# Widening float64 weights in an attention and expert kernel: the power of two taken from the moved upper word

## The chip, the cores and the metric

One core of a Trainium2 chip runs the whole program. The metric is the device time of one execution in microseconds; a kernel's time is the median of several executions.

## The reference, cut to what matters

Causal attention over 4 batches, 12 heads, 448 positions and 64 channels; then a block that multiplies by weights given in float64 (`w_theta`, `w_tok_r`, `w_tok_i`, `w_ch`); then a second attention over 4 experts with a gate.

```python
x = attention(q, k, v)                      # (4, 448, 768)
theta = x @ w_theta
zr, zi = x * np.cos(theta), x * np.sin(theta)
y = np.einsum('ts,bsd->btd', w_tok_r, zr) + np.einsum('ts,bsd->btd', w_tok_i, zi)
u = x + y
x = u + np.maximum(u @ w_ch, 0.0)
...
for e in range(4):                          # the second attention, expert by expert
    ye = softmax(causal(scale * (x @ wq[e]) @ (x @ wk[e]).T)) @ (x @ wv[e]) @ wo[e]
    out += (gate of e, among the best 2) * ye
```

The float64 weights reach the chip as pairs of 32-bit words. The products are made in two float32r parts, a rounded upper part (`hi`) and the rest (`lo`), with three matmuls for each product.

## The kernel before, in words

Work goes batch by batch, four times: the first attention (`attn1`, six pairs of heads), the dense block (`dense1`: theta, sine and cosine, transposes, mixing along the tokens, channel product, projections of the experts) and the second attention (`attn2`, two pairs of heads and the output product). The first attention of the next batch and the second one of the batch before are laid between the products of the dense block, so that TensorE has work while other engines prepare operands.

`Plan` (lines 126 to 478) sets the order. Every call of an engine in the kernel's text becomes a step with a cost (`Plan.cost`, lines 143 to 172), a due time and dependences. `Plan.issue` lays the steps out engine by engine by due time and by when inputs and buffers come free; for a step with several possible engines (`copy`, `combine`, `scale`, lines 284 to 296) it takes the one that would end first. What it emits is a fixed order for each engine. The table `K` (lines 489 to 493) holds the due times of the stages: `start` and `len0` for the first batch's dense block, `len` and `len3` for the others, `d1`, `g1` and `gap` for the attention beside them. A VectorE step of one source counts as fast, half the time for each column, by

```python
psum = any(v.root.psum for v in ins)
fast = name in ("tensor_scalar", "tensor_copy", "memset") and not psum and n >= 64
```

where `ins` are its inputs; the output is not looked at.

`widen` (lines 543 to 560) makes `hi` and `lo` of a tile of raw float64 words: 24 tiles of 384 columns for theta and channel weights (`c1`, shown as `c`), and 7 tiles of 448 for the token weights (`zt`, converted into `wt`). All of it is done in the first batch; `hi` and `lo` of the 24 go to DRAM (`scr`) and are loaded again by the later batches. Step by step: ScalarE scales the upper word (line 547), VectorE shifts it to its place and keeps the exponent (line 550) and adds the sign (line 552), both into `cmb`; VectorE masks the mantissa's bits in place (line 553); ScalarE makes of them a number from 1 to 2 in the PSUM tile `cv` (line 555); VectorE adds the lower word times 2^-52 (line 557); VectorE or POOL multiplies by the power of two (line 558); then come the rounded part and the difference (lines 559, 560), on whichever engine is first. `cv` is one PSUM bank, which the transposes ahead of the token mixing use too (lines 783 to 800).

In `dense1` each of the six theta products (`big`, line 747) fills one of two `mm` banks; VectorE's `zt<-mm` rows (lines 767, 768) empty it. Each of six token-mixing chains (lines 804 to 814) is 21 matmuls of `wt` with `zn`; `zn` is a transposed tile's rounded part and its residual, the VectorE row `zn<-cv,zn` of line 800. Names: `sc` scores, `pa`, `pc`, `zn` (in the first batch) their exponentials, `tp` and `ph` transposed ones, `hl` the two parts of an attention's output, `unit` the two parts of a weight tile. All instructions are recorded at line 478, so the trace is read by tiles.

Of the kernel before, what the change touches and what calls it, by code (L numbers as in the profile page):

```python
# [15 lines left out]
U32 = mybir.dt.uint32  # L16
AF = mybir.ActivationFunctionType
OP = mybir.AluOpType
# [13 lines left out]
LOWBIT = 2.0 ** -52  # L32
# [93 lines left out]
class Plan:  # L126
# [171 lines left out]
    def rank(self):  # L298
# [6 lines left out]
        for s in reversed(self.steps):  # L305
            if not s.users:
                continue
            path = s.lag if s.engine == "sync" else s.cost
            latest = min(u.due for u in s.users) - path * K["path"] - K["hop"]
            s.due = min(s.due, latest) if s.engine == "tensor" else latest  # L310

    def issue(self):
# [8 lines left out]
        def lag(e, d):  # L321
            if d == e:
                return OWN[e]
            return LATENCY[e] + K["slack"] + (50.0 if d == "tensor" else 0.0)

# [40 lines left out]
        def unpark(tag):  # L366
            for e, x in parked.pop(tag, ()):
                if not x[2].issued:
                    bisect.insort(avail[e], x, key=lambda x: x[:2])
# [5 lines left out]
        while count < len(self.steps):  # L375
# [13 lines left out]
            for e in order:  # L389
# [64 lines left out]
                for t in s.tiles:  # L454
                    t.left -= 1
                    if t.left == 0 and t.bufs:
                        heapq.heappush(free[t.tag], (done + K["war"], t.slot))
                        heapq.heappush(wake, done + K["war"])
                        unpark(t.tag)
# [21 lines left out]
class Engine:  # L481
# [3 lines left out]
    def __getattr__(self, method):  # L485
        return lambda *a, **kw: self._plan.add(self._name, method, *a, **kw)


K = {"path": 1.62, "hop": -40.0, "slack": 10.0, "war": 300.0, "ahold": 41390.0, "f1": 0.03, "f2": 0.79, "f3": 1.13,
# [4 lines left out]


# [1 line left out]
def dense_sparse_attention_kernel(ctx: ExitStack, tc: tile.TileContext, qk, v, w64, w32, wo, wvg, wtok, out):  # L497
# [6 lines left out]
    plan = Plan(nc, tc)  # L504
    pe, act, dve, pool, sp = (Engine(plan, n) for n in ("tensor", "scalar", "vector", "gpsimd", "sync"))
# [5 lines left out]
    def sbt(shape, dtype, tag):  # L511
        return plan.tile(sb, [P] + shape, dtype, tag, BUFS[tag])

    def pst(tag):
        return plan.tile(psp, [P, 512], F32, tag, PBUFS[tag], psum=True)
# [27 lines left out]
    def widen(raw, n, hi, lo):  # L543


        e_ = raw[:, :n, 1]
        act.activation(e_.f32(), e_.f32(), AF.Copy, scale=REBIAS)
        e_ = e_.bitcast(U32)
        p_ = sbt([S], F32, "cmb")[:, :n]
        dve.tensor_scalar(p_.bitcast(U32), e_, 3, 0x7F800000, op0=OP.logical_shift_left, op1=OP.bitwise_and)  # L550
        plan.claim(hi)
        dve.scalar_tensor_tensor(p_.bitcast(U32), e_, 0x80000000, p_.bitcast(U32), op0=OP.bitwise_and, op1=OP.bitwise_or)
        dve.tensor_scalar(e_, e_, 0xFFFFF, None, op0=OP.bitwise_and)
        x_ = pst("cv")[:, :n]
        act.activation(x_, e_, AF.Copy, scale=2.0 ** -20, bias=1.0)
        y_ = e_.bitcast(F32)
        dve.scalar_tensor_tensor(y_, raw[:, :n, 0].bitcast(U32), LOWBIT, x_, op0=OP.mult, op1=OP.add)
        plan.combine(p_, y_, p_, OP.mult, "vg")
        plan.copy(hi, p_, "sgv")
        plan.combine(lo, p_, hi.f32(), OP.subtract, "gv")  # L560

    def convert(src, n, hi, lo, tag="c1"):

        raw = sbt([S, 2], I32, tag)
        if src.dtype == F32:
            raw = raw.rearrange("p a b -> p (a b)").bitcast(F32)[:, :n]
            sp.dma_start(raw, src)
            plan.copy(hi, raw, "sgv")
            plan.combine(lo, raw, hi.f32(), OP.subtract)
        else:  # L570
            sp.dma_start(raw[:, :n].rearrange("p a b -> p (a b)"), src.bitcast(I32))
            widen(raw, n, hi, lo)
# [33 lines left out]
    def pair(raw, vts, gate, dest, due, gap, tag=lambda name: name):  # L606
# [18 lines left out]
        def part(j, c):  # L625
            return ps[j][:, SECS[c]:SECS[c] + 128 * (c + 1)]
# [18 lines left out]
        def norm(a, b_, items):  # L645
            dve.tensor_scalar(rec[:, a:b_], sums[:, a:b_], 1e-9, None, op0=OP.add)
            dve.reciprocal(rec[:, a:b_], rec[:, a:b_])
            if gate is not None:
                dve.tensor_tensor(rec[:, a:b_], rec[:, a:b_], gate[:, a:b_], op=OP.mult)
            for p, col in items:  # L650
                plan.scale(p, p, rec[:, col:col + 1])

        scores([2])
        norm(0, 2, [(part(j, 2), j) for j in range(2)])
        plan.due = due + K["f1"] * gap
        sc_ = pst("sc")
# [3 lines left out]
        norm(2, 7, [(pc[:, :S], 6)] + [(part(j, c), 2 * (2 - c) + j) for c in (1, 0) for j in range(2)])  # L660
        plan.due = due + K["f2"] * gap

# [280 lines left out]
    for b in range(B):  # L943
        gap = K["gap"] + (K["gap1"] if b == 1 else K["gap2"] if b == 2 else 0.0)
# [57 lines left out]
```

## Time and profile before

| what | value |
|---|---|
| median of 3 executions | 672.63 us (671.33 to 673.14) |
| the profiled execution, its own time | 672.36 us |
| its span, first to last instruction | 670.6 us |
| TensorE (PE) busy | 642.0 us, 96% of the span |
| VectorE (DVE) busy | 424.3 us, 63% |
| ScalarE (ACT) busy | 391.9 us, 58% |
| GpSimd (POOL) busy | 114.4 us, 17% |

A row's duration is longer than what it keeps its engine from the next: on VectorE the next row starts before the last one has ended. The start of the next row less the start of this one, on an engine that waits for nothing, is called its pitch below. TensorE's busy time counts overlapping matmuls once.

### The profile page before, as it was taken

Reading aid. Unit: us, or ns where it says so; the run is one execution under the profiler, and the core shown is the slowest. Engines: PE = TensorE matmul, PEld = TensorE weight load, DVE = VectorE, ACT = ScalarE, POOL = GpSimd, SP = SyncE. Lnnn points to the kernel's source line nnn. Section 1 sums busy time; section 2 is a strip of 40 time slices with the busy share of each in tenths; the row PEclk is TensorE's granted clock in tenths of the full one; section 3 lists DMA queues with packets and bytes.
Section 4 is the critical chain, followed back from the end, with each engine's and each line's share of the span. In section 5 each row is a group of like instructions: output and inputs, shape, how many; then the busy total and the mean of one; then the engine's idle time right before and its main releaser. Section 6 shows DMA issues by size and latency. Waiting matters only on the chain.

```text
span 670.6 us, 11048 instructions
## 1 busy us (share of the span) xinstructions
PE 642.0 (96%) x3728; PEld 520.5 (78%) x3728; DVE 424.3 (63%) x1325; ACT 391.9 (58%) x976; POOL 114.4 (17%) x224
## 2 busy tenths in 40 slices
PE   7997779999999999999999999999999999999987
PEld 5564567878797879887787778888878888998865
DVE  4999999999955685544526686553633567434251
ACT  5999788786813684444547677444555374105274
POOL 3542212222400120011001123001101012001010
PEclk9999789999999999999999999999999999999999
DMA  8846640355878624246546543415541750064253
GB/s 329 310 139 201 206 134 29 110 163 187 285 230 291 212 91 147 91 140 177 166 98 211 168 134 85 133 36 163 169 122 49 258 157 11 24 222 119 63 173 117
DMA packets 46184, 103.13 MB, mean 154 GB/s; under 512 B 4784, under 2 KB 16560, under 8 KB 46128
## 3 DMA queue, kind: packets, MB, share of 16 engines
q1 hardware_dynamic: 46128, 102.43, 48.0%
q8 instruction: 29, 0.48, 0.3%
q14 instruction: 27, 0.22, 0.1%
HBM read 81.15 MB, written 21.26 MB: 153 GB/s over the span
## 4 chain that ended last, share of the span: by engine, by line
PE 81%; DVE 8%; ACT 6%; DMA 3%; issue 1%; POOL 0%; ACTq 0%; SPq 0%; POOLq 0%; DVEq 0%
PE mm L478 53%; PE av L478 10%; PE sc L478 8%; PE tp L478 7%; PE cv L478 3%; DVE cmb L478 2%; ACT pa L478 2%; DMA unit<-scr 2%; ACT zn L478 1%; DVE zt L478 1%; DVE zn L478 1%; ACT ph L478 1%; DVE c L478 1%; ACT pc L478 1%; DVE pa L478 1%
## 5 line engine op out<-in xcount | busy, mean ns | idle before, releaser
L478 PE MATMUL mm<-zt,unit 128*128 128x448 f32 x720 | 161.4, 374 | 0.0
L478 ACT ACTIVATE pa<-pa,st 128x384 f32<-128x384 f32 (+2 forms) x265 | 126.6, 493 | 59.4 <-DVE st L478 55.3
L478 PEld LDWEIGHTS mm<-zt,unit 128*128 128x128 f32 x720 | 132.3, 188 | 16.6 <-issue 5.0
L478 PE MATMUL mm<-wt,zn 128*128 128x448 f32 x504 | 126.9, 380 | 0.6 <-ACT zn L478 0.5
L478 PE MATMUL mm<-hl,unit 128*128 128x448 f32 x432 | 102.8, 383 | 7.4 <-DVE zt L478 4.8
L478 PEld LDWEIGHTS mm<-wt,zn 128*128 128x128 f32 x504 | 90.0, 188 | 13.8 <-issue 3.1
L478 PEld LDWEIGHTS mm<-hl,unit 128*128 128x128 f32 x432 | 80.5, 192 | 21.2 <-DVE zt L478 6.6
L478 POOL TENSOR_SCALAR pa<-pa,st 128x384 f32<-128x384 f32 (+2 forms) x83 | 45.1, 551 | 267.6 <-DVE st L478 196.5
L478 DVE CUSTOM_DVE_ANT_0 pa<-sc,mask 128x384 f32<-128x384 f32 (+1 forms) x174 | 66.7, 418 | 36.8 <-PE sc L478 31.9
L478 ACT ACTIVATE ph<-tp 128x512 f32<-128x512 f32 x100 | 55.0, 593 | 29.8 <-PE tp L478 29.5
L478 PE MATMUL sc<-raw 64*128 64x384 f32 (+3 forms) x336 | 68.3, 432 | 1.4 <-DVE st L478 1.2
L478 PE MATMUL tp<-ident,pa 128*128 128x128 f32 x348 | 59.7, 279 | 5.0 <-POOL pa L478 5.0
L478 PEld LDWEIGHTS tp<-ident,pa 128*128 128x128 f32 x348 | 44.1, 143 | 12.9 <-POOL pa L478 6.6
L478 DVE TENSOR_TENSOR zn<-cv,zn 128x512 fp32r<-128x512 f32 (+1 forms) x48 | 29.8, 621 | 32.5 <-ACT zn L478 32.2
L478 PE MATMUL av<-ph,vt 128*64 128x448 f32 (+3 forms) x384 | 46.8, 386 | 2.2 <-ACT xt L478 2.2
L478 ACT ACTIVATE pc<-pc,st 128x448 f32<-128x448 f32 x51 | 34.1, 669 | 24.6 <-DVE st L478 23.9
L478 PEld LDWEIGHTS av<-ph,vt 128*64 128x64 f32 x384 | 25.4, 136 | 27.7 <-issue 13.3
L478 PEld LDWEIGHTS sc<-raw 64*128 64x128 f32 (+1 forms) x336 | 33.5, 187 | 12.4 <-issue 6.9
L478 PE MATMUL mm<-unit,zt 128*128 128x260 f32 (+1 forms) x264 | 36.9, 289 | 0.3 <-DMA unit<-scr 0.3
L478 PEld LDWEIGHTS mm<-unit,zt 128*128 128x128 f32 (+1 forms) x264 | 33.1, 183 | 4.2 <-issue 2.4
L478 ACT ACTIVATE zn<-cv 128x512 fp32r<-128x512 f32 (+1 forms) x34 | 18.5, 543 | 26.1 <-PE cv L478 25.9
L478 DVE SCALAR_TENSOR_TENSOR xt<-mm,xt 128x448 f32<-128x448 f32 x24 | 14.9, 620 | 29.3 <-PE mm L478 29.3
(121 smaller groups left out, 900.2 us busy)
## 6 DMA issues: line engine op xcount, KB each, us to landing
unit<-scr SPq DMA_DIRECT2D x96, 384.0 KB, 3.5
scr<-unit SPq DMA_DIRECT2D x32, 384.0 KB, 3.2
raw<-qk SPq DMA_DIRECT2D x24, 480.0 KB, 4.2
c<-w SPq DMA_DIRECT2D x24, 384.0 KB, 3.5
vt<-v SPq DMA_DIRECT2D x24, 256.0 KB, 2.9
unit<-scr SPq DMA_DIRECT2D x18, 260.0 KB, 3.1
c<-scr SPq DMA_DIRECT2D x18, 256.0 KB, 2.9
out<-cmb SPq DMA_DIRECT2D x18, 224.0 KB, 2.7
```

The source lines that it names most:

```text
L478: getattr(getattr(self.nc, engine), name)(*args, **kw)
```

## The change

In `widen` the shifted upper word keeps its mantissa bits too (mask `0x7FFFFFFF`), so that with the sign it is already the number without its lower word. Sign and exponent of it alone (mask `0xFF800000`) are a signed power of two, which VectorE writes to the PSUM tile `cv`. The lower word times 2^-52 times that power is added to the number. ScalarE's step on the mantissa (line 555 of before) is gone; VectorE's mask (line 553 of before) now reads `cmb` and writes `cv`.

```diff
-        dve.tensor_scalar(p_.bitcast(U32), e_, 3, 0x7F800000, op0=OP.logical_shift_left, op1=OP.bitwise_and)
+        dve.tensor_scalar(p_.bitcast(U32), e_, 3, 0x7FFFFFFF, op0=OP.logical_shift_left, op1=OP.bitwise_and)
...
-        dve.tensor_scalar(e_, e_, 0xFFFFF, None, op0=OP.bitwise_and)
         x_ = pst("cv")[:, :n]
-        act.activation(x_, e_, AF.Copy, scale=2.0 ** -20, bias=1.0)
+        dve.tensor_scalar(x_.bitcast(U32), p_.bitcast(U32), 0xFF800000, None, op0=OP.bitwise_and)
         y_ = e_.bitcast(F32)
-        dve.scalar_tensor_tensor(y_, raw[:, :n, 0].bitcast(U32), LOWBIT, x_, op0=OP.mult, op1=OP.add)
-        plan.combine(p_, y_, p_, OP.mult, "vg")
+        dve.scalar_tensor_tensor(y_, raw[:, :n, 0].bitcast(U32), LOWBIT, x_, op0=OP.mult, op1=OP.mult)
+        plan.combine(p_, y_, p_, OP.add, "vg")
```

The table `K` of due times changes in most of its numbers, among them:

```diff
-K = {... "ahold": 41390.0, "f2": 0.79, "start": 56960.0, "d1": 25290.0, "len0": 146150.0, "len": 108640.0 ...}
+K = {... "ahold": 48650.0, "f2": 0.91, "start": 57670.0, "d1": 24290.0, "len0": 118380.0, "len": 113780.0 ...}
```

Since the plan lays everything out anew, the order of nearly all instructions changes from the first widening on. VectorE at the first widening (`c_10` is a raw weight tile, `cmb_223` the number in the making):

```order
 L478 COPY ph_240<-tp_211 128x512
-L478 TENSOR_SCALAR c_10_83<-c_10_83 128x384
-L478 TENSOR_SCALAR cmb_255<-c_12_87 128x384
+L478 TENSOR_SCALAR cv_253<-cmb_223 128x384
+L478 TENSOR_SCALAR cmb_256<-c_12_87 128x384
+L478 SCALAR_TENSOR_TENSOR c_10_83<-c_10_83,cv_253 128x384
 L478 ISA zn_208,st_209<-sc_243,mask_67 128x256
 L478 ISA st_209 128x1
```

The row of the lower word follows the mask two rows later, where it came after a step of ScalarE before. VectorE at the residual for the fifth token-mixing chain (`zn_1584` before, `zn_1562` now), before:

```order
L478 TENSOR_SCALAR c_272_1098<-c_272_1098 128x384
L478 TENSOR_SCALAR cmb_1593<-c_276_1130 128x384
L478 CAST zn_1584<-cv_1583 128x512
L478 SCALAR_TENSOR_TENSOR cmb_1593<-c_276_1130,cmb_1593 128x384
L478 TENSOR_TENSOR zn_1584<-cv_1583,zn_1584 128x512
L478 TENSOR_TENSOR xt_657<-xt_657,mm_1492 128x448
```

and now:

```order
L478 TENSOR_SCALAR cv_1545<-cmb_1513 128x384
L478 SCALAR_TENSOR_TENSOR c_272_1079<-c_272_1079,cv_1545 128x384
L478 TENSOR_SCALAR cmb_1557<-c_317_1339 128x384
L478 TENSOR_TENSOR cmb_1513<-c_272_1079,cmb_1513 128x384
L478 TENSOR_TENSOR xt_727<-xt_727,mm_1493 128x448
L478 TENSOR_TENSOR zn_1562<-cv_1561,zn_1562 128x512
```

The rounded part of that tile has gone to ScalarE, and the row that empties the bank of the fourth chain (`xt`) stands ahead of the residual instead of behind it. TensorE at the same place, before:

```order
L478 MATMUL mm_1492<-wt_502,zn_1539 128x448 x5
L478 MATMUL tp_1601<-ident_111,pa_1215 128x2x64
L478 MATMUL tp_1601<-ident_111,pa_1350 128x2x64
L478 MATMUL tp_1601<-ident_111,pa_1215 128x2x64
L478 MATMUL tp_1601<-ident_111,pa_1350 128x2x64
L478 MATMUL mm_1607<-wt_502,zn_1584 128x448 x2
L478 MATMUL tp_1612<-ident_111,pa_1215 128x2x64
L478 MATMUL tp_1612<-ident_111,pa_1350 128x2x64
L478 MATMUL tp_1612<-ident_111,pa_1215 128x2x64
L478 MATMUL tp_1612<-ident_111,pa_1350 128x2x64
L478 MATMUL mm_1607<-wt_502,zn_1584 128x448 x10
```

and now:

```order
L478 MATMUL tp_1576<-ident_111,pa_1262 128x2x64
L478 MATMUL tp_1576<-ident_111,pa_1348 128x2x64
L478 MATMUL tp_1576<-ident_111,pc_1033 128x128
L478 MATMUL sc_1586<-raw_1029 128x384
L478 MATMUL sc_1587<-raw_1029 128x384
L478 MATMUL mm_1596<-wt_794,zn_1562 128x448
L478 MATMUL cv_1599<-ident_111,zt_1214 128x128 x3
L478 MATMUL mm_1596<-wt_794,zn_1562 128x448 x11
```

Other pieces of the attention beside it fill the places between the chain's matmuls.

## Rows read from the trace of the kernel before

**Rows 1.** Busy time by stretch: us, each engine's busy us (instructions), granted clock, DMA share.
```profile
20.00:61.00 41.00, 36.97 (x244) 24.42 (x240) 39.15 (x135) 40.47 (x118) 19.03 (x32) 1.00 0.62 208
61.00:98.00 37.00, 27.45 (x129) 20.38 (x130) 35.94 (x102) 28.09 (x66) 4.75 (x8) 0.86 0.56 183
98.00:132.00 34.00, 33.45 (x191) 27.30 (x192) 33.50 (x83) 27.38 (x59) 10.40 (x12) 1.00 0.20 67
180.00:640.00 460.00, 456.94 (x2660) 381.59 (x2659) 250.66 (x784) 228.78 (x564) 55.15 (x116) 1.00 0.46 141
640.00:670.60 30.60, 23.75 (x140) 18.01 (x138) 8.10 (x38) 17.61 (x42) 3.01 (x6) 1.00 0.49 159
```

**Rows 2.** VectorE's waits, 6 to 110 us: us in total, times, longest.
```profile
DVE zn L478 <- PE sc L478: 5.5, 3, 4.2
...
DVE st L478 <- ACT pa L478: 0.8, 1, 0.8
DVE xt L478 <- ACT hl L478: 0.7, 1, 0.7
DVE hl L478 <- ACT xt L478: 0.4, 1, 0.4
```

**Rows 3.** TensorE's waits, 6 to 120 us, the longest.
```profile
PE mm L478 <- DVE zt L478: 4.8, 3, 2.8
```

**Rows 4.** VectorE's timeline: start us, duration us, row.
```profile
93.55 0.39 DVE L478 TENSOR_SCALAR zt<-zt 128x448 uint32<-128x448 uint32 x1
93.85 0.39 DVE L478 TENSOR_SCALAR cmb<-zt 128x448 uint32<-128x448 uint32 x1
...
130.59 0.35 DVE L478 TENSOR_SCALAR c<-c 128x384 uint32<-128x384 uint32 x1
130.86 0.35 DVE L478 TENSOR_SCALAR cmb<-c 128x384 uint32<-128x384 uint32 x1
131.13 0.68 DVE L478 CAST zn<-cv 128x512 fp32r<-128x512 f32 x1
131.73 0.55 DVE L478 SCALAR_TENSOR_TENSOR cmb<-c,cmb 128x384 uint32<-128x384 uint32 x1
132.20 0.68 DVE L478 TENSOR_TENSOR zn<-cv,zn 128x512 fp32r<-128x512 f32 x1
132.80 0.61 DVE L478 TENSOR_TENSOR xt<-xt,mm 128x448 f32<-128x448 f32 x1
133.33 0.68 DVE L478 COPY ph<-tp 128x512 f32<-128x512 f32 x1
```

**Rows 5.** TensorE's timeline at the fifth chain, merged.
```profile
132.05 0.65 PE L478 MATMUL mm<-wt,zn 128*128 128x448 f32 x2
132.54 0.60 PE L478 MATMUL tp<-ident,pa 128*128 128x128 f32 x4
132.94 2.31 PE L478 MATMUL mm<-wt,zn 128*128 128x448 f32 x10
```

**Rows 6.** Groups by form: count, busy us, mean ns of one, idle ahead of them.
```profile
L478 DVE TENSOR_SCALAR zt<-mm 128x448 f32<-128x448 f32 x24 | 14.8, 617 | 17.2 <-ACT mm L478 17.1
L478 ACT ACTIVATE cv<-c 128x384 f32<-128x384 uint32 x24 | 12.6, 524 | 5.2 <-DVE c L478 4.4 <-DVE zn L478 0.8
L478 DVE TENSOR_SCALAR zt<-zt 128x448 uint32<-128x448 uint32 x31 | 12.0, 393 | 0.3
L478 DVE TENSOR_SCALAR c<-c 128x384 uint32<-128x384 uint32 x24 | 8.8, 365 | 0.0
L478 ACT ACTIVATE cv<-zt 128x448 f32<-128x448 uint32 x7 | 4.0, 573 | 1.8 <-DVE zt L478 1.1 <-DVE zn L478 0.6
```

**Rows 7.** Busy time by stretch, rows that touch `cv` alone; ScalarE's is the fourth.
```profile
20.00:61.00 41.00, 0.00 (x0) 0.00 (x0) 3.47 (x7) 3.68 (x7) 1.00 0.62 208
```

**Rows 8.** The chain that ended last, in order of time.
```profile
102.88 0.75 PE sc L478 x2
162.72 0.87 PE tp L478 x8
```

More of the change, by code (lines that the diff above doesn't have):

```diff
@@ L486, in __getattr__ @@
         return lambda *a, **kw: self._plan.add(self._name, method, *a, **kw)
-K = {"path": 1.62, "hop": -40.0, "slack": 10.0, "war": 300.0, "ahold": 41390.0, "f1": 0.03, "f2": 0.79, "f3": 1.13,
[3 rows of a table removed]
+K = {"path": 1.62, "hop": -40.0, "slack": 10.0, "war": 300.0, "ahold": 48650.0, "f1": 0.03, "f2": 0.91, "f3": 1.13,
[3 rows of a table added]
      "01v", "wom": "m", "wo2": "a", "warm": 24}
```

6 rows, old and new, of the table K are left out of this document.

## The prediction

> **What bounds the kernel now.** I read the busy time by stretch first, then the waits of VectorE and TensorE, then two timelines, then the groups by form. The stretches [rows 1] split the program in two. From 180 to 640 us TensorE is busy for 456.94 of 460 us while VectorE and ScalarE are about half busy: there only TensorE's own work counts, and the diff changes none of it. From 20 to 61 us ScalarE is busy for 40.47 of 41 us and VectorE for 39.15; from 61 to 98 us VectorE has 35.94 of 37, ScalarE 28.09, and TensorE only 27.45 at a granted clock of 0.86 of the full 2.4 GHz. So the first 130 us, in which the float64 weights are widened beside the first attention, are where a change of `widen` can be paid or earned, and VectorE is the engine with no room. The waits agree: between 6 and 110 us VectorE waits 5.5 us for the scores (one wait of 4.2 us is the start), and only 0.8, 0.7 and 0.4 us for ScalarE [rows 2]; TensorE waits 4.8 us in three pieces for VectorE's `zt` rows [rows 3]. From about 105 us on TensorE is full, but just in time: VectorE's residual for the fifth token-mixing chain runs from 132.20 to 132.88 us [rows 4], and the ten matmuls that read it start at 132.94 us [rows 5], with four transposes put in ahead of them. Whatever makes that residual later makes TensorE later by as much.
>
> **The change, part by part.** Pitches are the start of the next row less the start of this one on a full VectorE [rows 4]: a one-source row from SBUF to SBUF 0.27 us at 384 columns and 0.30 at 448; a row with two sources, or with a PSUM source, 0.47 at 384, 0.53 at 448, 0.60 at 512.
>
> *ScalarE loses 31 rows*, 12.6 us in 24 of them and 4.0 us in 7 [rows 6]. In 20 to 61 us it is 3.68 us, 7 rows [rows 7]. I cost this at nothing by itself: VectorE is as full in that stretch and alone full in the next. What it gives is shorter waits of VectorE for ScalarE, at most the 0.8 + 0.7 + 0.4 = 1.9 us of [rows 2], at least 0; I take half, **-0.9 us**.
>
> *The mask row changes its target.* VectorE keeps five rows in a widening before the split. The third wrote its own SBUF tile (365 ns at 384 columns) [rows 6] and now writes the PSUM tile `cv`. No row of this trace has VectorE writing PSUM, so it is bounded: below by the SBUF row, pitch 0.27 (0.30 at 448), above by a row that loses its speed to a PSUM operand. For that the trace has a pair at 448 columns: `zt<-zt` from SBUF 393 ns, `zt<-mm` from PSUM 617 ns [rows 6]; so pitch 0.47 (0.53). A gain below the SBUF row I exclude: the row has the same elements and still one source. I take the upper end, since the nearest row with one PSUM operand and the same kind of operation is the slow one.
>
> The Trainium skill, page "VectorE: DVE Perf Modes", section "What auto-detection actually checks", speaks against this change: the double rate for a 32-bit one-source row needs the source and the destination both in SBUF. By that rule the row is the slow one and the sum is the 675.4 us below; if only a PSUM source cost, it would be the fast one and 670.6. The pair of rows above shows it for a source; no run here shows it for a destination.
>
> *The order.* Lines 157 to 164 price a VectorE row as slow when an input is in PSUM and never ask for the output, so the new order is laid out as if these rows were fast, and the table `K` has other due times. All rows of all engines move, so I compare at one place: the residual for the fifth token-mixing chain, with 370 VectorE rows ahead of it before and 368 now. Counted by kind ahead of that row:
> - masks: 22 rows in SBUF go (15 x 0.27 + 7 x 0.30 = 6.15 us), 23 rows into `cv` come (16 x 0.47 + 7 x 0.53 = 11.23 us): +5.1 us. At the lower bound 16 x 0.27 + 7 x 0.30 = 6.42: +0.3.
> - more of other rows: widening of the theta and channel weights is further on by two low-word rows and a combining one (3 x 0.47) and a shift (0.27); six conversions out of SBUF (3 x 0.27, 3 x 0.30), which ScalarE or POOL had; two rows on a PSUM operand at 448 (2 x 0.53): 1.41 + 0.27 + 1.71 + 1.06 = 4.45 us.
> - fewer: three `ph<-tp` copies and a conversion at 512 (4 x 0.60), seven rows at 0.53 (five sums and differences, a conversion from PSUM, a score row), one score row of 0.47 and one conversion of 0.30: 2.40 + 3.71 + 0.47 + 0.30 = 6.88 us. Thirteen of the program's `ph<-tp` copies go to ScalarE in all, three of them here: that is how the plan spends what ScalarE was relieved of.
>
> VectorE reaches the place 5.1 + 4.45 - 6.88 = **+2.7 us** later (lower bound -2.1).
>
> *TensorE* has five rows less ahead of the same chain: a score of 448 columns (two instructions, 0.75 us) and four transposes (8 take 0.87 us, so 0.44) [rows 8]. These **1.2 us** are still to be done behind the place, where it is full.
>
> DMAs: SP's queue has 301 rows in both orders, with the same sizes; POOL has 228 instructions for 229, TensorE 3250 in both. I cost these at nothing; the cover is that TensorE's idle time from 180 to 640 us is 3.06 us in all [rows 1]. A wait that grew there would show at once, and I allow 2 us each way. The last 30.6 us (TensorE busy 23.75) keep TensorE's order row for row in the final 70 rows.
>
> Sum: +2.7 + 1.2 - 0.9 = +3.0 us. The profiled execution took 672.36 us (span 670.6), 0.27 below the median of 672.63. So **675.4 us**. With the wait term between 0 and -1.9 it is 674.4 to 676.3, with the 2 us each way 672.4 to 678.3.
>
> **Rivals.**
> - *VectorE writes PSUM at the SBUF speed.* Then -2.1 + 1.2 - 0.9 = -1.8 us, 670.6 (669.6 with all waits gone). For it: no row here shows such a write. Against: the 617 ns row.
> - *ScalarE sets the pace at the start* (the other side). It is busy 40.47 of 41 us in 20 to 61 us [rows 1]; if the plan's chain there runs through its exponentials, the 3.68 us of `cv` rows [rows 7] come off that stretch, and VectorE's added rows find room because its inputs come sooner: 672.36 - 3.7 = 668.7. It decides if VectorE's waits for the score rows, which depend on ScalarE through the recycled tiles, are more than the 1.9 us I count. Against: VectorE is full for 35.94 of 37 us afterwards, where nothing that comes sooner helps.
> - *The order slips further.* A plan that counts 31 rows too cheaply by 0.2 us each puts every consumer of `hi` and `lo` too early; if TensorE's queue is blocked behind such rows and later work can't pass, all 24 x 0.20 + 7 x 0.23 = 6.4 us are lost and not 5.1, with no gain of waits: 672.36 + 6.4 - 2.4 + 1.2 + 2 = 679.6.
> - That the change computes something else can hardly be: a power of two with its sign times the lower word, added to the moved word, is the same number, and counts of matmuls and DMAs are equal.
>
> **How the numbers follow.** Forecast 0.55; fast PSUM writes 0.20; ScalarE's pace 0.15; further slip 0.10. A measurement of this kernel tells about 0.3% from no change, 2.0 us: faster is below 670.6, slower above 674.6. ScalarE's case is faster (0.15), half of the fast writes (0.10) and a little of the forecast (0.02): 0.27. The other half of the fast writes and a third of the forecast's spread (0.19) are no difference: 0.29. The rest is slower: 0.44. Signs are mixed, so the forecast's own range, 672.4 to 678.3, stands beside the whole one: 668.5 (ScalarE's case) to 679.0 (just short of the slip).
>
> **What the next profile would show.** `cv<-cmb` at 384 columns near 0.55 us, not 0.36, and 31 of them. VectorE at 36 us or more of 37 in 61 to 98 us; the fifth chain's residual at about 134 us, not 132.2; ScalarE with idle time in 20 to 61 us. TensorE full from about 108 us and its idle time behind 180 us near 3 us. I am wrong if the write takes 0.36 us, if VectorE shows idle time between 61 and 98 us, or if a wait on a DMA or on `zn` of over 2 us stands behind 180 us.

## The result and the profile after

| | median, us | lowest to highest | executions |
|---|---|---|---|
| before, beside it | 672.18 | 671.33 to 673.14 | 4 |
| changed | 679.37 | 677.89 to 680.43 | 4 |
| changed, measured again later (e16) | 678.75 | 676.88 to 680.85 | 6 |

Changed over before is 1.0106 (95% interval 1.0084 to 1.0129), and 1.0087 (1.0068 to 1.0107) the second time: slower by 6 to 7 us where +3.0 was forecast. The profiled execution took 680.07 us with a span of 678.3, so 7.7 more than the one of before in both.

The busy time by stretch of the changed kernel, with the columns of [rows 1]:

```profile
20.00:61.00 41.00, 38.87 (x258) 25.04 (x256) 40.28 (x138) 39.48 (x116) 17.91 (x31) 1.00 0.70 234
61.00:98.00 37.00, 26.53 (x123) 19.73 (x120) 35.68 (x94) 23.74 (x57) 11.56 (x15) 0.77 0.46 151
98.00:132.00 34.00, 30.37 (x157) 24.18 (x156) 32.51 (x74) 18.81 (x36) 8.03 (x8) 0.90 0.15 43
180.00:640.00 460.00, 457.27 (x2672) 381.94 (x2671) 251.21 (x779) 238.21 (x584) 57.77 (x120) 1.00 0.46 141
640.00:678.30 38.30, 31.15 (x189) 23.93 (x187) 12.63 (x64) 22.02 (x60) 3.01 (x6) 0.98 0.39 127
```

From 180 to 640 us TensorE is as full as before (457.27 of 460), and the last stretch is longer only because work was left for it. All of the loss arises earlier. In 98 to 132 us TensorE, 33.45 busy before, is at 30.37, and its mean granted clock there and in the stretch ahead fell from 1.00 and 0.86 to 0.90 and 0.77. ScalarE lost its rows (23.74 and 18.81 us, for 28.09 and 27.38) and VectorE stayed full: 35.68 of 37.

The groups by form on VectorE, as in [rows 6]:

```profile
L478 DVE TENSOR_SCALAR cv<-cmb 128x384 uint32<-128x384 uint32 x24 | 13.2, 550 | 0.0
L478 DVE TENSOR_SCALAR cmb<-c 128x384 uint32<-128x384 uint32 x24 | 8.4, 352 | 0.0
L478 DVE TENSOR_SCALAR cv<-cmb 128x448 uint32<-128x448 uint32 x7 | 4.3, 619 | 0.0
```

The mask row that writes PSUM takes 550 ns at 384 columns. The shift, of the same shape and kind from SBUF to SBUF, takes 352. This is the price that the prediction took.

TensorE's waits from 6 to 180 us, the longest, and its timeline:

```profile
PE mm L478 <- DVE zt L478: 8.9, 2, 8.2
PE sc L478 <- DVE st L478: 3.4, 4, 1.2
PE cv L478 <- DVE zn L478: 1.4, 1, 1.4
```

```profile
88.29 9.87 PE L478 MATMUL mm<-hl,unit 128*128 128x448 f32 x36 [8.19 <-DVE zt L478]
...
104.17 0.90 PE L478 MATMUL cv<-ident,zt 128*128 128x128 f32 x3 [1.42 <-DVE zn L478]
...
136.69 0.63 PE L478 MATMUL cv<-ident,zt 128*128 128x128 f32 x4 [0.48 <-DVE c L478]
...
138.97 0.47 PE L478 MATMUL mm<-wt,zn 128*128 128x448 f32 x1
```

Where three waits for `zt` made 4.8 us [rows 3], one of 8.2 stands: the fourth theta product needs the bank of the second, which VectorE empties with two rows, from 86.74 us on, from 81.16 before. The fifth token-mixing chain starts at 138.97 us; it started at 132.05 [rows 5]. The wait of 0.48 ahead of 136.69 is one for the PSUM bank `cv`, which a widening row of VectorE (`c<-c,cv`, from 135.99 us) still reads.

VectorE's timeline, first where POOL has its three products (the second fence is POOL's), then at the residual of the fifth chain:

```profile
96.17 0.62 DVE L478 SCALAR_TENSOR_TENSOR zt<-zt,cv 128x448 f32<-128x448 uint32 x1
96.70 1.41 DVE L478 TENSOR_TENSOR wt<-cmb,wt 128x448 fp32r<-128x448 f32 x1
98.03 1.56 DVE L478 TENSOR_TENSOR cmb<-zt,cmb 128x448 f32<-128x448 f32 x1
99.52 2.08 DVE L478 TENSOR_TENSOR zt<-zt,xt 128x448 f32<-128x448 f32 x2
101.53 0.38 DVE L478 TENSOR_SCALAR cmb<-zt 128x448 uint32<-128x448 uint32 x1
...
137.20 0.62 DVE L478 TENSOR_TENSOR xt<-xt,mm 128x448 f32<-128x448 f32 x1
137.99 0.69 DVE L478 TENSOR_TENSOR zn<-cv,zn 128x512 fp32r<-128x512 f32 x1 [0.17 <-ACT zn L478]
```

```profile
96.47 4.11 POOL L478 TENSOR_TENSOR zt<-zt,xt 128x448 f32<-128x448 f32 x3 [2.71 <-ACT zt L478]
```

Beside POOL's rows the four VectorE rows with two sources in SBUF go on for 4.83 us (96.70 to 101.53), where four pitches of 0.53 are 2.1: 2.7 us are lost. The Trainium skill, page "SBUF — State Buffer", section "Who interferes with whom", says that such a VectorE row contends with a GpSimd instruction that reads SBUF, and that the ports which the two share are an exclusive lock. The rows agree: pitches of 1.33 and 1.49 us are about one POOL row (4.11 / 3 = 1.37).

The residual is at 137.99 us for 132.20 [rows 4], +5.8. The start accounts for 0.7 of this: VectorE's first wait for scores was 4.2 us [rows 2] and is 4.9 here, and it lies between 4.0 and 4.9 in the profiles of all kernels. So VectorE's way to the residual is compared below from the end of that first wait: 130.6 us here, 125.5 before, +5.1 where the prediction had +1.8. How much of it VectorE is busy, the third busy time of these lines tells (before, then the changed kernel):

```profile
6.71:132.20 125.49, 109.46 (x631) 79.25 (x632) 119.67 (x366) 107.59 (x277) 37.77 (x59) 0.96 0.53 183
```

```profile
7.42:137.99 130.57, 111.38 (x620) 79.99 (x620) 124.42 (x364) 97.38 (x254) 44.09 (x65) 0.91 0.52 180
```

Its rows take 4.8 us more (124.42 for 119.67), where the prediction's rows summed to +2.7, and the stretched rows beside POOL are 2.7 of the 4.8. Its idle time is 6.1 us for 5.8, where the prediction took off 0.9.

### The profile page after: what moved, and what is told of

The parts are those of the page before. It is cut to its first block, busy times and chain, and to the rows that moved or that the text cites. A ratio compares the mean times of both kernels' runs of the same rounds, so it can differ in the third digit from the quotient of the medians.

```text
span 678.3 us, 11033 instructions
## 1 busy us (share of the span) xinstructions
PE 646.4 (95%) x3728; PEld 523.6 (77%) x3728; DVE 428.9 (63%) x1318; ACT 381.2 (56%) x953; POOL 116.5 (17%) x223
## 4 chain that ended last, share of the span: by engine, by line
PE 75%; DVE 14%; ACT 7%; issue 2%; DMA 1%; POOL 0%; ACTq 0%; DVEq 0%; POOLq 0%
PE mm L478 50%; PE av L478 9%; PE sc L478 8%; PE tp L478 6%; DVE zt L478 3%; DVE cmb L478 3%; PE cv L478 2%; ACT pa L478 2%; DVE cv L478 1%; DVE pa L478 1%; DVE zn L478 1%; ACT zn L478 1%; DVE c L478 1%; ACT zt L478 1%; ACT ph L478 1%
## 5 line engine op out<-in xcount | busy, mean ns | idle before, releaser
L478 PE MATMUL mm<-zt,unit 128*128 128x448 f32 x720 | 163.6, 376 | 0.2 <-DVE xt L478 0.2
L478 PE MATMUL mm<-wt,zn 128*128 128x448 f32 x504 | 125.3, 380 | 0.5 <-DVE zn L478 0.5
L478 PE MATMUL mm<-hl,unit 128*128 128x448 f32 x432 | 105.2, 393 | 12.2 <-DVE zt L478 10.3
L478 PEld LDWEIGHTS mm<-hl,unit 128*128 128x128 f32 x432 | 83.6, 200 | 24.4 <-DVE zt L478 11.1
L478 ACT ACTIVATE ph<-tp 128x512 f32<-128x512 f32 x113 | 62.6, 594 | 52.6 <-PE tp L478 52.4
L478 POOL TENSOR_SCALAR pa<-pa,st 128x256 f32<-128x256 f32 (+2 forms) x82 | 44.3, 549 | 208.8 <-DVE st L478 157.6
L478 PE MATMUL sc<-raw 64*128 64x384 f32 (+3 forms) x336 | 69.7, 441 | 3.5 <-DVE st L478 3.4
L478 ACT ACTIVATE pc<-pc,st 128x448 f32<-128x448 f32 x57 | 38.0, 667 | 27.6 <-DVE st L478 25.2
L478 ACT ACTIVATE zn<-cv 128x384 fp32r<-128x384 f32 (+1 forms) x38 | 20.4, 537 | 36.8 <-PE cv L478 36.7
L478 ACT ACTIVATION_READ_ACCUMULATOR pa<-pa,st 128x1 f32 x174 | 32.8, 189 | 0.0
```

The costliest lines, as they stand in the source:

```text
L478: getattr(getattr(self.nc, engine), name)(*args, **kw)
```

## Experiments

The theories at first were: the mask rows in PSUM are most of the loss; or the order is. Times are medians of 4 to 12 executions, ratios those to the kernel before on the same chip. "Way" is VectorE's time from its first score row to the fifth chain's residual, in the one profile of each kernel (before 125.5), so tenths of it are not to be trusted: the changed kernel's two profiles differ by 0.5.

| run | order | mask row | median, us | ratio (95%) | way, us |
|---|---|---|---|---|---|
| changed / e16 | new | PSUM | 679.37 / 678.75 | 1.0106 / 1.0087 (above) | 130.6 / 130.0 |
| e1 | new | SBUF | 676.30 | 1.0037 (1.0024 to 1.0050) | 126.9 |
| e2 | old, ScalarE's rows kept | slow, SBUF | 676.03 | 1.0038 (1.0024 to 1.0052) | 127.9 |
| e15 | old | slow, SBUF | 677.71 | 1.0066 (1.0049 to 1.0083) | 127.7 |
| e9 | old | PSUM | 679.46 | 1.0099 (1.0083 to 1.0115) | 129.6 |
| e10 | old | SBUF | 672.28 | 0.9991 (0.9979 to 1.0004) | 123.8 |
| e13 | new, products on VectorE | SBUF | 675.54 | 1.0025 (1.0007 to 1.0042) | 124.6 |
| e6 | new, products on VectorE | PSUM | 676.95 | 1.0053 (1.0035 to 1.0071) | 128.5 |

### The mask row's target, in the order of before (e2, e15, e9, e10)

In e9 and e10 the plan lays out the kernel before, and the calls are exchanged when they are emitted, so that every other row stays in its place. The new mask row takes the place of ScalarE's in e9, and that of the old mask in e10; the other rows of the new arithmetic are as in the change. e10:

```diff
         dve.tensor_scalar(e_, e_, 0xFFFFF, None, op0=OP.bitwise_and)
+        plan.steps[-1].calls[-1] = ("vector", "tensor_scalar", (e_, p_.bitcast(U32), 0xFF800000, None), {"op0": OP.bitwise_and})
         x_ = pst("cv")[:, :n]
         act.activation(x_, e_, AF.Copy, scale=2.0 ** -20, bias=1.0)
+        plan.steps[-1].calls.pop()
+        x_.root.alias = raw[:, :, 1].bitcast(F32)
```

In e9 the first of the added lines is a `pop()`, and the call with target `x_` replaces ScalarE's. In e15 the mask is `scalar_tensor_tensor` with `p_` as a second source, which makes it slow without PSUM. In e2 the arithmetic of before stays and its old mask row is made slow in that way:

```diff
         dve.tensor_scalar(e_, e_, 0xFFFFF, None, op0=OP.bitwise_and)
+        plan.steps[-1].calls[-1] = ("vector", "scalar_tensor_tensor", (e_, e_, 0xFFFFF, e_), {"op0": OP.bitwise_and, "op1": OP.bitwise_and})
```

e2: 

> The kernel before with its order kept; the 31 mask rows read their tile twice as a two-source row, so each takes 0.47/0.53 us of VectorE instead of 0.27/0.30 and computes the same. Theory 1 (VectorE has no room in the first 130 us): 22 rows ahead of the fifth chain add 4.9 us, so 676.5 to 678.5 us against 672.2. Rival (the old order has slack that hides them, and only the new order is sensitive): 674 or less.

e9: 

> The whole change of the arithmetic, with the mask row writing PSUM and without ScalarE's 31 rows, but in the order of before, row for row. If the slow rows are one part of the loss and the new order the other: 674.5 to 677, as with the slow row alone, less up to 1.9 for ScalarE's rows. If the loss comes from the arithmetic in any order: 678 to 681.

e10: 

> The same with the mask row writing the raw word in SBUF: the change without its slow rows and without its new order. If these two are all there is: 670 to 673, no slower than before, and up to 1.9 us faster by shorter waits for ScalarE. If the arithmetic costs something besides (rows with two sources in SBUF next to POOL's): 674 to 677.

e15: 

> The change in the order of before with the mask row in SBUF, without ScalarE's rows, but the row made a slow one by giving it a second source. If the rate of the row is what costs: 678 to 680, as with the row that writes PSUM in that order. If the bank that the PSUM row holds costs on top (TensorE's transposes wait for it): 674.5 to 676.5, as with the slow row beside ScalarE's rows.

The groups by form of the mask row in e9, e15 and e10, one fence each:

```profile
L478 DVE TENSOR_SCALAR cv<-cmb 128x384 uint32<-128x384 uint32 x24 | 13.3, 553 | 0.0
```

```profile
L479 DVE SCALAR_TENSOR_TENSOR c<-cmb 128x384 uint32<-128x384 uint32 x24 | 13.5, 562 | 0.0
```

```profile
L479 DVE TENSOR_SCALAR c<-cmb 128x384 uint32<-128x384 uint32 x24 | 8.7, 361 | 0.0
```

e10 is level with before (0.9991) and e9 is 1.0099, the whole loss, in the order of before. TensorE, ScalarE and POOL have the same rows in the same order in the two. They differ in the target of one VectorE row and in where that row stands: in e9 it comes 0 to 21 VectorE rows later than in e10, 2 in the median. So **the target, with the place that goes with it, makes a change that costs nothing into one that costs about 7 us** (0.0108 of 672.8), and the reading that the order is half of the loss, which stood after e1 and e2, falls: with some 2.5 us each they had fitted it, each between its two expectations, but e9 has no new order. Of e9's two expectations the one for two parts, 674.5 to 677, was missed, and the one for the arithmetic in any order, 678 to 681, came.

How much of the 7 us is the rate of the row? e15 has a row as slow (562 ns) and gives 1.0066, 5.0 us more than e10, between its two expectations; e2, with ScalarE's rows still there, gives 2.6 more than before. (Their slow row has two sources in SBUF and can meet POOL's rows as those at 96.70 us did; a mean of 562 ns leaves little for that.) The rest, 2 to 4 us, comes with PSUM or with the later place of the row. The two intervals of e15 and e9 just meet at 1.0083, so this part is likely and not certain. What it could be, the timeline of TensorE in e9 shows:

```profile
131.98 0.52 PE L478 MATMUL cv<-ident,zt 128*128 128x128 f32 x3 [0.23 <-DVE c L478]
...
143.13 0.55 PE L478 MATMUL cv<-ident,zt 128*128 128x128 f32 x3 [0.39 <-DVE c L478]
...
153.01 0.52 PE L478 MATMUL cv<-ident,zt 128*128 128x128 f32 x3 [0.25 <-DVE c L478]
```

The transposes ahead of the token mixing wait for the one `cv` bank until VectorE's row has read the power of two out of it: 0.9 us in three waits, which neither before nor e10 nor e15 has. In before ScalarE filled that bank, so it was held too, but no such wait shows. From the residual to 180 us TensorE is idle for 1.4 us in e9 (41.99 busy of 43.43), 0.2 in e15 and 0.1 in before, 0.6 of the 0.9 among the 1.4. The remainder of the 2 to 4 is not explained.

### The order (e1, e3, e4, e7, e8, e6, e13)

e1 keeps the changed kernel's order and only redirects `x_` to the raw word's place in SBUF when it is emitted:

```diff
         x_ = pst("cv")[:, :n]
+        x_.root.alias = raw[:, :, 1].bitcast(F32)
         dve.tensor_scalar(x_.bitcast(U32), p_.bitcast(U32), 0xFF800000, None, op0=OP.bitwise_and)
```

e3 is the kernel before with the new `K`, e4 the changed one with the old `K`. e7 and e8 let the plan itself lay out the mask row in SBUF, with the new and the old `K`:

```diff
-        x_ = pst("cv")[:, :n]
-        dve.tensor_scalar(x_.bitcast(U32), p_.bitcast(U32), 0xFF800000, None, op0=OP.bitwise_and)
+        x_ = e_.bitcast(F32)
+        dve.tensor_scalar(e_, p_.bitcast(U32), 0xFF800000, None, op0=OP.bitwise_and)
```

e1: 

> The changed kernel with every engine's order kept, only the mask row's target moved: the 31 VectorE rows write the upper words of the raw tile in SBUF instead of the PSUM tile. Theory 1 (the rows into PSUM are the loss): pitch 0.27/0.30 us instead of 0.47/0.53, 6.4 us less VectorE work, 4.9 us of it ahead of the fifth token-mixing chain, and TensorE's 8.2 us wait gets shorter by what stands ahead of it; 672 to 674.5 us against 679.4. Rival (the new order is the loss, whatever these rows take): 677.5 or more.

e3: 

> The widening of before, with the changed kernel's table of due times: the program has none of the slow mask rows, only the order that the other due times give. Theory 1 (the loss is mostly the mask rows in PSUM): 671.5 to 674, no difference from before. Theory 2 (most of the loss is the order, which puts the evacuation of the second theta product behind more widening): 674.5 to 677, with a wait of TensorE for zt of 7 us or more in two pieces.

e4: 

> The changed widening with the table of due times of before. Theory 1: as slow as the changed kernel, 678 to 681, since the 31 mask rows are still slow. Theory 2: the due times of before take back the wait at the second theta product, 674 to 677. Counted by the rows that VectorE and TensorE have ahead of each chain, this order needs VectorE 4.8 us earlier than the changed kernel's does: by that count 683 to 688.

e7: 

> The changed widening with the masked word written over the raw word in SBUF, laid out by the plan itself (which now prices this row rightly), with the changed kernel's due times. Theory 1: the rows ahead of the fifth token-mixing chain come 1.9 us sooner than in before, so 670 to 672.5; the mask row's target was the change's one real fault. Rival (ScalarE's 31 rows were never worth anything and the moved rows cost as much as they give): 673 to 676.

e8: 

> As the run before, with the due times of before. By the rows ahead of each chain VectorE comes 1.8 us later than in before: 673 to 675. If the wait at the second theta product follows from the due times and not from the rows, it is the 5 us of before here and 8 us with the changed kernel's.

| run | widening | `K` | median, us | ratio (95%) |
|---|---|---|---|---|
| e3 | before | new | 676.22 | 1.0043 (1.0030 to 1.0056) |
| e4 | changed | old | 683.66 | 1.0150 (1.0130 to 1.0169) |
| e7 | changed, SBUF | new | 677.10 | 1.0063 (1.0043 to 1.0083) |
| e8 | changed, SBUF | old | 679.89 | 1.0100 (1.0083 to 1.0116) |

All four lay-outs other than that of before are slower, with the arithmetic of before too (e3, +2.9 us) and with fast mask rows (e7 +4.2, e8 +6.7). The count of rows ahead of the chains had e7 at 670 to 672.5 and e8 at 673 to 675: it is no measure of what an order costs. Only e4, which that count put at 683 to 688, came as said. e3 lies where the second theory put it, but without the wait that was to be its reason: TensorE waits 1.3 us for `zt` there. e1 against e10, the same arithmetic and the same fast rows in the two orders, gives **3.1 us for the new order** (0.0046 of 672.8), where the prediction's count of moved rows gave a gain of 2.4. It holds at equal mean granted clock: at 0.985 e1 took 676.3 and 676.8 us, e10 672.3 to 673.9. With slow rows the two orders are level (e9 1.0099; changed 1.0106 and 1.0087): the losses do not add, and why is open.

e6 and e13 move POOL's three products to VectorE when they are emitted, in the changed kernel and in e1:

```diff
+            engine = "vector" if step.mark else engine
...
                     plan.combine(z[:, 0], z[:, 0], xt[j], OP.mult)
+                    plan.steps[-1].mark = b == 0 and m == 2
```

e6: 

> The changed kernel with POOL's three back-to-back products of the first batch (96.5 to 100.6 us) put on VectorE at the same place of the order. Theory 3 (beside them three two-source VectorE rows have pitches of 1.3 to 1.5 us instead of 0.53, a loss of 2.7 us): three rows more cost VectorE 1.6 us and the three get 2.7 us shorter, so 678 to 679 us, and no VectorE row of 448 columns over 0.7 us near 98 us. Rival (the long rows come from something else): they stay, and the time is 680.5 to 681.

e13: 

> The changed kernel's order with the mask row in SBUF and the three products on VectorE in place of POOL, which had stretched VectorE's rows beside them. If the order costs about 3 us only through such stretched rows: 672 to 674, level with before. If it costs by where it puts the rows that TensorE waits for: 675 to 677, as with the mask alone undone.

e13's VectorE, at the place where the rows were stretched:

```profile
93.73 0.62 DVE L481 TENSOR_TENSOR wt<-cmb,wt 128x448 fp32r<-128x448 f32 x1
94.27 0.62 DVE L481 TENSOR_TENSOR cmb<-zt,cmb 128x448 f32<-128x448 f32 x1
94.80 1.15 DVE L481 TENSOR_TENSOR zt<-zt,xt 128x448 f32<-128x448 f32 x2
95.87 0.39 DVE L481 TENSOR_SCALAR cmb<-zt 128x448 uint32<-128x448 uint32 x1
```

The pitches are 0.53 again, and although VectorE has three rows more its way is 2.3 us shorter than in e1 (124.6 for 126.9) and 2.1 shorter in e6 (128.5 for 130.6). At the end e6 is 2.3 to 3.6 us below the changed kernel, more than its expectation had; e13's median is only 0.8 below e1's, which their intervals do not tell apart.

e13's median hides two groups. Five of its executions, with a mean granted clock of 0.992, took 672.06 to 673.34 us, level with before; seven, at 0.984 and 0.985, took 675.19 to 677.20; none lies between. So each of its two expectations came in a part of the executions, and **the same program in the same order differs by some 3.5 us with the clock**. Its profile is of the first group (672.74 us) and has TensorE's wait for the second theta product's bank all the same (8.1 us, as in e1): there that wait costs nothing at the end. That the order costs by where it puts the rows TensorE waits for is thus not shown. What is shown is the stretched rows; what puts an execution into one group or the other no run tells, nor whether the clock is the cause there or follows from waits that differ.

### TensorE's clock (e5, e11, e12, e17, e18) and copies on ScalarE (e14)

TensorE's busy time and granted clock (the columns behind the stretch: length, busy, clock), in before and then in the changed kernel:

```profile
60.00:70.00 10.00, 6.12 (x34) 0.86 0.69 236
70.00:80.00 10.00, 10.00 (x52) 0.80 0.41 133
80.00:90.00 10.00, 6.77 (x28) 0.83 0.81 261
90.00:100.00 10.00, 6.56 (x30) 1.00 0.20 64
100.00:110.00 10.00, 9.51 (x55) 1.00 0.00 0
```

```profile
60.00:70.00 10.00, 8.16 (x39) 0.80 0.48 151
70.00:80.00 10.00, 9.55 (x57) 0.86 0.62 203
80.00:90.00 10.00, 1.81 (x7) 0.65 0.71 237
90.00:100.00 10.00, 10.00 (x46) 0.83 0.00 1
100.00:110.00 10.00, 6.91 (x26) 0.68 0.01 2
```

Busy time times what the clock lacks to 1.00 is 4.0 us in before (6.12 x 0.14 + 10.00 x 0.20 + 6.77 x 0.17) and 7.5 in the changed kernel, by the same product over its five rows. The fall to the lower level, 1.2 of 2.4 GHz, comes each time behind or in a wait of TensorE: near 67 and 84 us in before, where waits end at 68.43 and 83.09, and near 66, 83 and 104 us in the changed kernel, where they end at 64.72, 88.29 and 104.17. The prediction has no term for it. To see what it costs, transposes of the identity into a PSUM tile that is free or is overwritten next, of which nothing is used, were put ahead of instructions that wait: 64 at the longest wait in e5, 89 at four places in e11, 95 and 79 in the kernel before in e12 and e17, 79 in e10 (this is e18):

```diff
+    FILL = {249: 3, 251: 3, 255: 18, 302: 24, 322: 16, 324: 9, 342: 6}
...
+            if engine == "tensor":
+                self.fill(args[0].root)
```

e5: 

> The changed kernel with 64 transposes of the identity added on TensorE ahead of the fourth theta product, where it waits 8.2 us for VectorE. Theory 2 (part of the loss is TensorE's granted clock, 0.74 to 0.83 from 80 to 120 us): the clock stays at full speed through the wait, the 57 matmuls of 88 to 98 and 106 to 112 us take some 4 us less, and the time falls to 675 to 677.5 us. Rival (VectorE alone sets the pace and TensorE's speed there is hidden): 679 to 680; if the added transposes outlast the wait, 681 or more.

e11: 

> The changed kernel with transposes of the identity put into TensorE's four longest waits between 80 and 106 us (64, 8, 12 and 5 of them), so that it does not idle there. If the lower clock behind those waits is a term of its own: 674 to 676, 2.4 us below the run with one fill, since the stretch at half clock behind 104 us goes as well. If it is not: 677 to 678.5.

e12: 

> The kernel before with such transposes in its waits between 59 and 98 us (94 of them). Its trace has 4.5 us lost to the lower clock there. If these lie behind waits for VectorE, which end when they end: 671.5 to 674, no change. If they are on the path: 667.5 to 670, faster than both kernels.

e17: 

> The kernel before with 79 transposes of the identity in six of its waits between 63 and 98 us, without the 16 that had run behind a wait and not in it and had put VectorE 2.9 us back. If the half clock there lies behind TensorE's waits for VectorE and POOL: 672 to 674, no change. If a part of it is on the path: 670 to 671.5, some 1.5 us or more below before.

e18: 

> The change with the mask row in SBUF, in the order of before, with the same 79 transposes. If both give what they can: 669 to 671, faster than both kernels. If VectorE's place and the clock are hidden by other waits: 671.5 to 673.5.

| run | on top of | median, us | ratio (95%) |
|---|---|---|---|
| e5 | changed | 677.34 | 1.0065 (1.0048 to 1.0082) |
| e11 | changed | 678.63 | 1.0089 (1.0070 to 1.0107) |
| e12 | before | 673.29 | 1.0000 (0.9987 to 1.0012) |
| e17 | before | 671.12 | 0.9977 (0.9968 to 0.9985) |
| e18 | e10 | 670.81 | 0.9971 (0.9960 to 0.9982) |
| e14 | e10 | 672.45 | 0.9995 (0.9980 to 1.0011) |

In e12 one fill was misplaced: it wrote the `av` bank whose release was itself the wait, and so ran behind it.

```profile
61.82 3.20 PE L474 MATMUL av<-ident 128*128 128x128 f32 x16 [2.13 <-ACT xt L493]
64.95 2.34 PE L493 MATMUL av<-ph,vt 128*64 128x448 f32 x16
```

This put VectorE's way back by 2.2 us (127.7 for 125.5), and e12 says nothing. Without that fill, e17 is 1.6 us below before, with VectorE's way unchanged (125.7): a part of the half-clock time lies on the path in before. e17's profile still has a clock of 0.83 from 60 to 70 us, by the same product 1.4 of the 4.0 us (8.10 x 0.17), so 1.6 us are gained for 2.6 taken away. e18 has the full clock throughout in its profile (0.994 to 1.000 in the mean of each of its executions):

```profile
60.00:70.00 10.00, 8.78 (x60) 1.00 0.70 234
70.00:80.00 10.00, 9.33 (x65) 1.00 0.52 161
80.00:90.00 10.00, 8.54 (x48) 1.00 0.80 253
90.00:100.00 10.00, 9.40 (x55) 1.00 0.09 38
100.00:110.00 10.00, 9.43 (x56) 1.00 0.01 2
```

**e18 is faster than both kernels**: 2.0 us below before (1.2 to 2.7 by its interval), 8 to 9 below the changed one. Before with the same fills (e17) is level with it, so what e18 gains over before comes from the fills and not from the change. For the changed kernel the fills leave the question open. They raised the mean granted clock, 0.981 to 0.989 in its ten executions, to 0.989 to 0.992 in e5 and 0.989 to 0.997 in e11; but e5 and e11, which has e5's fill and three more, lie 1.6 us apart in the wrong sense, and e11 missed its expectation of 674 to 676. What the clock adds to the loss is between nothing and some 3 us.

e14 gives six of VectorE's copies to ScalarE, where e10 has room, by an exchange at emission (`wt` and `ph` copies, `tensor_copy` to `activation`):

```diff
+                if tag == "wt" and self.swap[tag] > 1 or tag == "ph" and 9 <= self.swap[tag] <= 10:
+                    engine, name, args = "scalar", "activation", (*args, AF.Copy)
```

e14: 

> The change with the mask row in SBUF in the order of before, and six of VectorE's copies between 61 and 140 us given to ScalarE, which has room there without its 31 rows: 6 rows of 0.30 and 0.60, some 2.4 us, off VectorE. If VectorE's place is all that sets the end: 669.5 to 671.5, faster than both kernels. If TensorE is bound there by other waits by now: 672 to 674.

It is no different from e10. VectorE's way was no longer what set the end there, or the copies were worth less (its way is 124.8 us, not shorter than e10's 123.8).

e16, the changed kernel again: 

> The changed kernel again, unchanged, beside the other three: 677.5 to 680. A second profile tells whether the stretches at half clock and the stretched rows are there each time.

The time came as said. Its profile has the stretched rows again (a pair of products of 2.08 us at 99.12 us) and a wait of 9.1 us for `zt`; of the stretches at half clock the one near 70 us is missing (1.00 from 60 to 80 us), those between 80 and 110 us are there.

## Why the prediction was wrong

The direction was right, the size was not: +3.0 was forecast, 6 to 7 were measured, and 679.37 lies above the range's 679.0 (the second measurement, 678.75, within it). VectorE's way takes the prediction's terms apart, in one profile of each kernel:

| term | forecast, us | on the way, us | from |
|---|---|---|---|
| ScalarE's rows gone | -0.9 | -1.7 | e10 less before |
| the mask row's target | +5.1 | +5.8 | e9 less e10 |
| the order | -2.4 | +0.9 (+0.4 with e16) | changed less e9 |

The order has the largest miss. By the prediction's steps:

- *The order, +4.45 - 6.88.* **This is the step that failed.** "I compare at one place" by a count of rows, each at its pitch, and set 2.4 us of gain against the mask rows. The new order gives no gain. One reason is shown: the pitches do not hold beside POOL, whose three products now fall on VectorE rows with two sources in SBUF (2.7 us; undone, VectorE's way is 2.1 to 2.3 shorter). That the engine of a row changes was counted, but not whom it runs beside. The count itself was near, as far as it goes: of the 4.8 us by which VectorE's rows grew, 2.1 remain without the stretch, for a summed 2.7. But VectorE's rows to one place do not give the end. There the new order costs 3.1 us with fast rows (e1 against e10) and nothing with slow ones, and such counts missed e7 and e8 by some 5 to 7 us. Without this credit the sum is +5.4, 677.8 us.
- *The mask row changes its target, +5.1 us.* Right in its price, too small in its sum. The row took the upper price (550 ns for a foreseen 550), and the slow rate costs 5.0 us at the end (e15 against e10; 2.6 in e2). The target costs 7.3 there (e9 against e10); the 2.2 more have no term in the prediction. The rule of the Trainium skill, page "VectorE: DVE Perf Modes", section "What auto-detection actually checks", that the double rate needs source and destination in SBUF, is now shown for a destination. **Fast PSUM writes**, a chance of 0.20, fell.
- *ScalarE loses 31 rows, -0.9 us.* In the order of before they shorten VectorE's way by 1.7 us (e10, 123.8 for 125.5) and give 0.6 at the end, which the measurement does not tell from nothing. In the new order the gain did not come: VectorE's idle time on the way is 6.1 us for 5.8. The rival by which ScalarE sets the pace fell with e10: its rows are gone there and the time is the same.
- *TensorE, 1.2 us left behind the place.* Not shown. In the changed kernel the residual is 5.8 us later, the chain 6.9, the end 7.7, so 1.9 are lost behind the residual. But e1, with the same order of TensorE, takes 538.3 us from its residual to the end, before 538.4; and e9, with the order of before, takes 541.0. The rows moved do not account for it by themselves. With rows into PSUM the stretch is 540.3 to 541.0 us in four profiles (changed, e16, e6, e9), but 538.9 and 539.1 with the fills of e5 and e11; what the 1.9 us come from is open.
- *DMAs and the stretch behind 180 us at nothing.* Right: 2.73 us idle of 460, for 3.06 before.
- Two terms were missing: the bank `cv`, for which TensorE now waits on VectorE (0.9 us in e9, and likely part of the 2 to 4 us by which PSUM costs more than its rate), and the clock, up to some 3 us.
- *The order slips further* named 679.6, near what came, but not its cause; that the time fits is luck. TensorE's queue does stand behind a late row, 8.2 us at the second theta product's bank; yet e1 has that wait (8.1) and is at +2.5, an execution of e13 with it is level with before, and e9 has the whole loss in the order of before with waits of 4.1 at most. What was right in it is that VectorE's waits became no shorter.

The prediction's own tests spoke in part: the mask rows at 0.55 us and TensorE full behind 180 us confirmed the first term, while the residual at 137.99, with "about 134" foreseen, showed that more was lost ahead of it. None of its three signs of being wrong appeared; they asked for a fast write, an idle VectorE or a late wait, and not for rows that take longer than their pitch.

## What to carry to other kernels

When a row moves from ScalarE to a full VectorE, look first at where it writes: here the same row into the raw word's place in SBUF cost nothing and into PSUM about 7 us, and a planner that prices rows by their inputs alone does not see it. (A plan that prices the row into PSUM rightly was not run.) A new order is not the sum of its rows' pitches: check which rows with two SBUF sources now run beside POOL, and test the arithmetic in the old order before judging it in a new one. Look at the granted clock of each execution before explaining a median: e13's was the middle of two groups. Where TensorE has to wait in a stretch with work to follow, spare transposes in the wait can be worth more than a rearrangement (1.6 us in the kernel before, nothing certain in the changed one).

## What the runs showed of the hardware

VectorE's write to PSUM costs as much as a read from it: 619 ns at 448 columns, for 617 of a read [rows 6]; at 384 it takes 550 to 553, for 352 to 365 from SBUF to SBUF. Beside POOL's two-source products the pitch of VectorE's two-source rows rose from 0.53 to 1.33 and 1.49 us at 448 columns (1.34 and 1.48 in the second profile of the changed kernel). TensorE's granted clock fell to 0.50 in or behind waits and stayed there for some microseconds into the work that followed (the 36 matmuls at 88.29 us took 9.87 us; 18 such take 3.92 at full clock, as at 97.86 us in before); with the waits filled it stayed at 1.00 in e18's profile. One program (e13) took 672.06 to 673.34 us in executions with a mean clock of 0.992 and 675.19 to 677.20 in those with 0.984 and 0.985.
